# Block-sparse attention and a gated MLP on one core: the order of the first loads and casts, and four groups of transposes

## The chip, the cores and the metric

One Trainium2 chip; the kernel runs on 1 of its cores, in one launch. The metric is the device time of one execution in microseconds, as a median of runs. All inputs lie in HBM as float32, the output goes back to HBM as float32; on the core nearly all products take bf16 operands.

## What is computed

Two layers, one after the other. The first is attention with a block mask, for 4 batches, 8 heads, 768 positions of 64 elements. The mask is the same for all heads; it lets a query block of 32 see its neighbours, the first and last block, and three sampled blocks.

```python
scores = scale * np.matmul(q, k.transpose(0, 1, 3, 2))
...
scores = np.where(mask, scores, -1000000000.0)
attn = softmax(scores)          # over the keys
x = (attn @ v), heads side by side: (4, 768, 512)
```

The second is a gated MLP with a mix over positions:

```python
h = np.maximum(x @ w_in, 0.0)                      # 768 x 1024 per batch
u, v = h[..., :512], h[..., 512:]
v_n = (v - mean(v)) / np.sqrt(var(v) + 1e-06)
v_s = np.einsum('ts,bsd->btd', w_spatial, v_n) + b_spatial[None, :, None]
out = (u * v_s) @ w_out
```

## The kernel before

**Tiles.** Two heads make a pair; there are 16 pairs, four to a batch. `load` (line 103) fetches a pair's k, q or v as 128 partitions x 2 heads x 384 float32 elements (384 KB) into a ring of three buffers for each of the three, and `cast` (115) turns it into bf16: k and q side by side in `nat`, 12 chunks of 128 columns (6 of k, 6 of q), v in `vv` with a column of ones. TensorE transposes `nat` chunk by chunk into PSUM, and VectorE copies it to `kq`, which holds for each of 8 heads 768 columns of k and 768 of q; its 24 further partitions hold the mask rows: block indicators on the k side, 0 or a large negative number on the q side. A score product over 88 rows thus masks as it multiplies. `rows` (239) copies these mask rows from head 0 to other heads.

**Stages.** The first batch (pairs 0 to 3) is worked by units, each a third of the queries (256) of one pair, `UNITS` at line 387; pair 0 is split by heads first. A unit has three slots. In a slot `qk_unit` (390) makes 128x1024 scores by four matmuls and one exponential of ScalarE. `av_unit` (438) follows some slots later with 8 matmuls per slot, and after a unit's third one VectorE normalizes it to `xn`. From slot 36 on heads are worked whole: `qk_full` (413) makes 128x768 scores per slot and `av_full` (465) takes 6 matmuls per slot, seven slots later. The x of a pair has to be transposed once more (`xt`) for the MLP: by TensorE and a copy of VectorE (`xtr_pe`, 485; `xtr_third`, 492, for a unit) or by a DMA transpose on SP's queue (`xtr_dma`, 500). The steps of the MLP (`Moe`, 556) are matmuls into one of two PSUM banks (`moe_tag`, 257, alternates them) and are dealt between the attention's slots by `run_queue` (684). The third batch's MLP runs beside the fourth batch's attention, and the last one by itself at the end.

**Order.** Nothing is scheduled automatically: each engine runs its instructions in program order, and waits are semaphores. The order of a slot is written out in the loop at line 807: scores, then `pre`, then attention products, then the steps under `at` (filled by `when`), then `run_queue`, then `late`. SP issues nearly all loads, stores and DMA transposes, strictly in program order; an issue that has to wait for a buffer holds up all behind it. Two loads of the first pair are issued by ScalarE.

**The start.** Head 0 of pair 0 comes first and in parts: four of six chunks of k and q (`C03`), so that the first scores need little data. The lines that the change touches:

```python
load(0, "k", H0, C03, eng=nc.scalar)
load(0, "q", H0, C03, eng=nc.scalar)
nc.sync.dma_start(out=samp[MR], in_=_listify(sampled_blocks).bitcast(I32))
...
cast(0, "k", nc.scalar, H0, C03)
rows(H1, K_, nc.scalar)
rows(slice(2, 3), slice(0, 512), nc.scalar)
cast(0, "q", PL, H0, C03)
```

`filler` (180) issues matmuls on zeros that are not read. `mask_rows` (272) makes the q side's mask rows for one third of the queries by a matmul and a copy. `split0` (284) copies half of a transposed group to `kq`. `tr_first` (348, slots 4, 7 and 10 for pairs 1, 2 and 3) transposes a pair's six chunks of k and the first two of q; `tr_rest` (356, slots 8, 11 and 14) the other four of q. From pair 4 on k and q are transposed by `tr_dma` (375) and copied by `split` (379), VectorE's copy of `tt` to `kq`.

Of the kernel before, what the change touches and what calls it, by code (L numbers as in the profile page):

```python
# [17 lines left out]
def _listify(ap: bass.AP) -> bass.AP:  # L18
    t = ap.tensor
    if isinstance(t.shape, tuple):  # L20
        t = dataclasses.replace(t, shape=list(t.shape))
        ap = dataclasses.replace(ap, tensor=t)
    return ap
# [3 lines left out]
def kernel(  # L27
# [35 lines left out]
    TC = NCH // NT  # L63
    TW = TC * 128
    S0 = NT * NG * 3
    FILL, FILL2, FILL3 = 26, (6, 0, 2), 4
    U_DVE = (0, 1, 2, 3)

    const = ctx.enter_context(tc.tile_pool(name="const", bufs=1))
# [27 lines left out]
            "h (p c) d -> p h (c d)", c=NCH)[:, :, cs.start * D:cs.stop * D]  # L97

    H0, H1, BOTH = slice(0, 1), slice(1, 2), slice(0, 2)
    ALLC, C01, C03, C45 = slice(0, NCH), slice(0, TC), slice(0, 2 * TC), slice(2 * TC, NCH)  # L100
    SRC = {"k": k, "q": q, "v": v}

    def load(p, nm, hs=BOTH, cs=ALLC, eng=nc.sync):
        if (nm, p) not in st:
            st[nm, p] = work.tile([128, 2, S // 2], FP32, tag="st_" + nm, bufs=3, name="st_" + nm)
        eng.dma_start(out=st[nm, p][:, hs, cs.start * D:cs.stop * D],  # L106
                      in_=dram(SRC[nm], p, hs, cs))
# [7 lines left out]
    def cast(p, nm, eng, hs=BOTH, cs=ALLC):  # L115
        if nm == "v":
            dst = vv[p % NVV][:, hs, cs, 0:D]
        else:
            if p not in nat:
                nat[p] = work.tile([128, 2 * NCH, 2, D], BF16, tag="nat", bufs=4, name="nat")  # L120
            c0 = 0 if nm == "k" else NCH
            dst = nat[p][:, c0 + cs.start:c0 + cs.stop].rearrange("p c h d -> p h c d")[:, hs]
        src = st[nm, p].rearrange("p h (c d) -> p h c d", d=D)[:, hs, cs]
        if p == 0 and nm != "v":
            dst = nat0_view()[:, hs, (c0 + cs.start) * D:(c0 + cs.stop) * D]
            if cs is not C45:
                dst = dst[:, 0].rearrange("p (i t d) -> p t i d", t=2, d=D)
                src = src[:, 0].rearrange("p (t i) d -> p t i d", t=2)
            else:
                dst = dst.rearrange("p h (c d) -> p h c d", d=D)  # L130
        if eng is nc.scalar:
            nc.scalar.activation(out=dst, in_=src, func=AF.Copy)
        else:
            eng.tensor_copy(out=dst, in_=src)  # L134

    samp = const.tile([KR, 2 * NR], I32)
    load(0, "k", H0, C03, eng=nc.scalar)
    load(0, "q", H0, C03, eng=nc.scalar)
    nc.sync.dma_start(out=samp[MR], in_=_listify(sampled_blocks).bitcast(I32))
    load(0, "k", H0, C45)  # L140
    load(0, "k", H1)
    load(0, "q", H1, C03)
    load(1, "k")
    load(1, "q")
    load(0, "v")
    load(2, "k")
    load(2, "q")
    load(1, "v")


# [29 lines left out]
    def filler(n, to):  # L180
        for _ in range(n):
            nc.tensor.matmul(out=to[:, 0:128], lhsT=warm, rhs=warm, start=True, stop=True)
# [56 lines left out]
    def rows(hs, cs, eng=nc.vector):  # L239
        src = kq[MR, 0:1, cs].to_broadcast([NB, hs.stop - hs.start, cs.stop - cs.start])  # L240
        if eng is nc.scalar:
            nc.scalar.activation(out=kq[MR, hs, cs], in_=src, func=AF.Copy)
        else:
            eng.tensor_copy(out=kq[MR, hs, cs], in_=src)

    cast(0, "k", nc.scalar, H0, C03)
    rows(H1, K_, nc.scalar)
    rows(slice(2, 3), slice(0, 512), nc.scalar)
    cast(0, "q", PL, H0, C03)
    cast(0, "k", PL, H0, C45)  # L250
    cast(0, "k", PL, H1)
    cast(0, "q", PL, H1, C03)


# [2 lines left out]
    def moe_tag():  # L257
        moe_tags.rotate(1)
        if moe_tags[0] in held:
            moe_tags.rotate(1)  # L260
        return moe_tags[0]
# [10 lines left out]
    def mask_rows(ps, t0, n, copy, rs=slice(0, KR)):  # L272
        nc.tensor.matmul(out=ps[:, 0:n * TW], lhsT=bm[rs],
                         rhs=kq[rs, 0, t0 * TW:(t0 + n) * TW], start=True, stop=True)
        return lambda: copy(kq[MR, 0, qcols(t0, n)], ps[0:NB, 0:n * TW])


    def head(ps, h, c0, n, at=0):
        for i in range(0, n, 2):
            nc.tensor.transpose(out=ps[:, at + i * 64:at + (i + 2) * 64],  # L280
                                in_=nat0_view()[:, h, (c0 + i) * D:(c0 + i + 2) * D],
                                identity=ident)

    def split0(ps, h, c0, n, t, copy=dve_copy):
        w = n * 64
        copy(kq[0:D, h, c0 * 128 + t * w:c0 * 128 + (t + 1) * w], ps[t * D:(t + 1) * D, 0:w])
# [2 lines left out]
    ps0 = bank()  # L289
    head(ps0, 0, *K4)  # L290
    split0(ps0, 0, *K4, 0)
    split0(ps0, 0, *K4, 1)
    filler(FILL2[0], wps)
    psq = bank("psq", "av")
    head(psq, 0, *Q4)
    split0(psq, 0, *Q4, 0)
    filler(FILL2[1], wps)
    mask_rows(psum.tile([128, 1024], FP32, tag="sc", bufs=2, name="mq"), 0, 1, act_copy)()
    m1 = mask_rows(psum.tile([128, 512], FP32, tag=moe_tag(), bufs=1, name="mq"), 1, 1, act_copy)
    m2 = mask_rows(psum.tile([128, 1024], FP32, tag="sc", bufs=2, name="mq"), 2, 1, dve_copy, MR)  # L300
    filler(FILL2[2], wps)
    split0(psq, 0, *Q4, 1)
    m1()
    m2()
    rows(H1, qcols(0, NT), PL)
    rows(slice(2, 3), slice(512, S), PL)

    cast(1, "k", PL)
    cast(1, "q", PL)
    cast(0, "v", PL)  # L310
    load(3, "k")
    cast(2, "k", PL)
    cast(2, "q", PL)
    cast(1, "v", PL)
    load(3, "q")
    cast(3, "k", PL)
# [175 lines left out]
    def xtr_third(u):  # L492
        t, p = UNITS[u]
        if t == "h":
            if p == 1:
                xtr_pe(0, xn_ref.pop(0), 0, 2 * TC)
        else:
            xtr_pe(p, xn_ref.pop(u), t * TC, TC, x_ref.pop(u))

    def xtr_dma(p):  # L500
        nc.sync.dma_start_transpose(
# [200 lines left out]
        return lambda: f(*a, **kw)  # L702

    K_Q0 = slice(0, S + TW)
    ROWS = [(1, 2, 8, qcols(0)), (1, 3, 4, K_), (5, 4, 6, K_), (6, 6, 8, K_), (14, 4, 8, qcols(1, 2))]
    when(0, second)
    when(1, third)
    when(2, lambda: filler(FILL3, psum.tile([128, 512], FP32, tag=moe_tag(), bufs=1, name="wps")))
# [4 lines left out]
    for p, sl in ((1, 8), (2, 11), (3, 14), (0, 17)):  # L713
        when(sl, c(tr_rest, p, 2 if p == 0 else 1))
    for u in range(1, len(UNITS)):
        late.setdefault({1: 13, 2: 13}.get(u, 3 * u + 7), []).append(c(xtr_third, u))

    def moe_begin(b):
        moe[b] = Moe(b)
# [59 lines left out]
    for p in range(NG, NP):  # L779
        g = slot_of(p)  # L780
        when({4: 14, 5: 22, 6: 31}.get(p, g - 34), c(load, p, "k"), c(load, p, "q"), c(load, p, "v"))
        when({4: 18, 5: 26, 6: 38}.get(p, g - 25),
             c(cast, p, "k", PL), c(cast, p, "q", PL), c(cast, p, "v", PL))
        when({4: 22, 5: 30}.get(p, g - 20), c(tr_dma, p))
        when(g - 5, c(split, p, 0))
        when(g - 3, c(split, p, 1))
        if p == NP - 1:
            when(g + 20, last_x)
        elif p % NG == NG - 1:
            when(g + 20, lambda p=p: xtr_pe(p, xn_ref.pop(("p", p)), 0, NCH))  # L790
        else:
            when(g + 20, c(xtr_dma, p))
    for i, (ld, ca) in enumerate([(16, 19), (16, 21), (17, 23), (17, 25), (23, 27), (23, 29)]):
# [65 lines left out]
```

## Time and profile before

| What | Value |
|---|---|
| Median of 3 runs | 214.83 us (214.56 to 215.42) |
| The profiled execution's own time | 215.21 us |
| Its span on the page | 213.4 us |
| Granted clock of TensorE, mean of the span | 0.99 |
| Busy: PE, ACT, DVE, POOL | 206.6, 171.0, 131.9, 72.9 us |
| DMA | 41.70 MB, mean 195 GB/s |

The profile shows one execution. Times in its views are microseconds from the start of the span unless marked ns. PE is TensorE's matmul row, PEld its weight loads, DVE is VectorE, ACT ScalarE, POOL GpSimd, SP the engine that issues DMAs. A row of a timeline has the start, the length from the first start to the last end, engine, line of the code, operation, out<-in by the program's names, shapes, the number of instructions merged into it, and in brackets the idle time of the engine before it and what ended it. The 1.8 us between span and own time lie around the span and are not resolved.

### The profile page before, as it was taken

To read this page: it belongs to the slowest core of one execution; us is meant where nothing else is said; L and a number is where in the kernel's file an instruction comes from. 1 tells how busy PE (TensorE), PEld (TensorE's weight loads), DVE (VectorE), ACT (ScalarE), POOL (GpSimd) and SP (SyncE) were. 2 spreads that over 40 slices of the span, in tenths; PEclk is the share of its full clock that TensorE was granted. 3 is DMA by queue.
4 is the path that set the end of the run, shared out by engine and by line. 5 is a ranking of instruction groups with operands and counts; after the bars stand their busy time and mean duration, and the time that the engine had idled before them with its cause. 6 is when DMAs were issued, how large, how long until landed. Compare 5 with 4: busy or idle time off the path is not lost.

```text
span 213.4 us, 5299 instructions
## 1 busy us (share of the span) xinstructions
PE 206.6 (97%) x2151; PEld 130.9 (61%) x2151; DVE 131.9 (62%) x287; ACT 171.0 (80%) x226; POOL 72.9 (34%) x119
## 2 busy tenths in 40 slices
PE   8799999999999999999999999999999999999992
PEld 7578887866666665665665565566656656544441
DVE  7589875988854535385887445286784433476551
ACT  6969999999999899979989788978989787266021
POOL 6589669867572405042442040130120000012000
PEclk9969999999999999999999999999999999999999
DMA  5999799999999999999691497697100324610265
GB/s 161 345 342 332 249 316 218 340 191 326 266 375 190 292 191 299 236 280 304 127 259 37 73 289 172 198 307 116 37 3 19 67 52 94 235 55 0 51 172 200
DMA packets 62780, 41.70 MB, mean 195 GB/s; under 512 B 44580, under 2 KB 57508, under 8 KB 62756
## 3 DMA queue, kind: packets, MB, share of 16 engines
q1 hardware_dynamic: 62324, 40.97, 74.7%
q10 hardware_dynamic: 432, 0.39, 0.6%
q8 instruction: 17, 0.28, 0.5%
q14 instruction: 7, 0.06, 0.1%
HBM read 24.38 MB, written 6.29 MB: 144 GB/s over the span
## 4 chain that ended last, share of the span: by engine, by line
PE 92%; DMA 3%; SPq 1%; ACT 1%; POOL 0%; DVE 0%; issue 0%; ACTq 0%
PE ps_moe L546 33%; PE ps L419 22%; PE ps_av L470 13%; PE ps_t L546 7%; PE ps L406 7%; PE ps_av L452 4%; PE ps_sc L546 4%; DMA st_q<-in_q_dram 3%; PE ps L267 1%; SPq L106 1%; PE ps_av L267 1%; ACT osb L217 0%; POOL nat L134 0%; ACT a_all L423 0%; DVE xn L435 0%
## 5 line engine op out<-in xcount | busy, mean ns | idle before, releaser
L423 ACT ACTIVATE a_all<-ps 128x768 bf16<-128x768 f32 x144 | 113.9, 812 | 14.9 <-PE ps L419 7.4
L419 PE MATMUL ps<-kq 88*128 88x384 bf16 x288 | 70.5, 325 | 0.1
L470 PEld LDWEIGHTS <-a_all 128*128 128x128 bf16 x864 | 46.5, 97 | 20.0
L470 PE MATMUL ps_av<-vv,a_all 128*128 128x65 bf16 x864 | 51.2, 194 | 0.0
L419 PEld LDWEIGHTS <-kq 88*128 88x128 bf16 x288 | 28.0, 98 | 31.0 <-issue 0.9
L546 PE MATMUL ps_moe<-w_in_t,xt 128*128 128x512 bf16 x144 | 44.0, 378 | 0.0
L411 ACT ACTIVATE a_all<-ps 128x1024 bf16<-128x1024 f32 x36 | 35.1, 1025 | 3.4 <-PE ps L406 2.9
L546 PE MATMUL ps_moe<-vn,w_spt 128*128 128x512 bf16 x108 | 32.7, 378 | 0.0
L134 POOL CAST nat<-st_k 128x768 bf16<-128x768 f32 (+2 forms) x17 | 13.6, 802 | 41.1 <-DMA st_k<-in_k_dram 40.8
L434 DVE RECIPROCAL rc<-ps_av 128x6 f32<-128x6 f32 (+1 forms) x36 | 6.7, 185 | 28.2 <-PE ps_av L470 26.6
L614 DVE SCALAR_TENSOR_TENSOR un<-ps_moe,b_col,un 128x512 bf16<-128x512 f32 x18 | 13.5, 750 | 16.7 <-PE ps_moe L546 16.1
L406 PE MATMUL ps<-kq 88*128 88x256 bf16 (+1 forms) x140 | 22.9, 286 | 0.7 <-ACT a_all L411 0.7
L583 POOL TENSOR_SCALAR std<-mv 128x3 f32<-128x3 f32 (+1 forms) x9 | 2.1, 238 | 62.2 <-DVE mv L580 45.5
L546 PE MATMUL ps_moe<-w_out_t,gt 128*128 128x512 bf16 x72 | 21.5, 378 | 0.0
L546 PEld LDWEIGHTS <-xt 128*128 128x128 bf16 x192 | 15.4, 97 | 7.2 <-DVE xt L214 0.2
L435 DVE TENSOR_TENSOR xn<-ps_av,rc 128x384 bf16<-128x384 f32 (+1 forms) x36 | 18.5, 513 | 1.2
L579 DVE BATCH_NORM_STATS2 stats<-vn 128x6 f32<-128x512 bf16 x24 | 16.5, 687 | 1.4 <-ACT vn L574 0.9
L134 POOL CAST nat<-st_q 128x768 bf16<-128x768 f32 (+1 forms) x18 | 14.1, 782 | 6.9 <-DMA st_q<-in_q_dram 6.5
L406 PEld LDWEIGHTS <-kq 88*128 88x128 bf16 x140 | 12.8, 100 | 4.6 <-issue 0.8
L134 POOL CAST vv<-st_v 128x768 bf16<-128x768 f32 x16 | 13.6, 855 | 5.7 <-DMA st_v<-in_v_dram 5.6
L452 PEld LDWEIGHTS <-a_all 128*128 128x128 bf16 x288 | 14.2, 100 | 2.0 <-issue 0.7
L214 DVE COPY kq<-tt 64x1536 bf16<-64x1536 bf16 x24 | 15.0, 627 | 0.3
(84 smaller groups left out, 211.8 us busy)
## 6 DMA issues: line engine op xcount, KB each, us to landing
st_v<-in_v_dram SPq DMA_DIRECT2D x16, 384.0 KB, 6.0
out_dram<-osb SPq DMA_DIRECT2D x23, 256.0 KB, 3.1
st_k<-in_k_dram SPq DMA_DIRECT2D x15, 384.0 KB, 4.4
st_q<-in_q_dram SPq DMA_DIRECT2D x15, 384.0 KB, 5.4
ws_f<-in_moe_w_spatial_dram SPq DMA_DIRECT2D x6, 384.0 KB, 6.6
w_f<-in_moe_w_in_dram SPq DMA_DIRECT2D x8, 256.0 KB, 5.9
w_f<-in_moe_w_out_dram SPq DMA_DIRECT2D x4, 256.0 KB, 4.2
st_q<-in_q_dram SPq DMA_DIRECT2D x2, 128.0 KB, 4.7
```

The costliest lines, as they stand in the source:

```text
L134: eng.tensor_copy(out=dst, in_=src)
L214: nc.vector.tensor_copy(out=o, in_=i)
L406: nc.tensor.matmul(out=ps[:, at:at + n * TW], lhsT=kq[:, h, ci * 128:(ci + 1) * 128], rhs=kq[:, h, qcols(t0, n)], start=True, stop=True)
L411: nc.scalar.activation(out=out, in_=ps, func=AF.Exp, scale=0.125)
L419: nc.tensor.matmul(out=ps[:, hf * 512:hf * 512 + HALF], lhsT=kq[:, j % H, ci * 128:(ci + 1) * 128], rhs=kq[:, j % H, S + hf * HALF:S + (hf ...
L423: nc.scalar.activation(out=a_ref["h", j][:, ci, :].rearrange("p (b c) -> p b c", b=2), in_=ps.rearrange("p (b c) -> p b c", b=2)[:, :, 0:H ...
L435: nc.vector.tensor_tensor(out=out, in0=ps[:, :, 0:D], in1=rc[:, 0:n].to_broadcast([128, n, D]), op=ALU.mult)
L452: nc.tensor.matmul(out=av_ref[u][:, to, :], lhsT=a_ref[u][:, at:at + 128], rhs=vv[pp % NVV][:, h, ci, :], start=(ci == 0), stop=(ci == NCH ...
L470: nc.tensor.matmul(out=av_ref[j][:, qc, :], lhsT=a_ref["h", j][:, ci, qc * 128:(qc + 1) * 128], rhs=vv[p % NVV][:, h, ci, :], start=(ci == ...
L546: nc.tensor.matmul(out=ref["ps"][:, 0:w], lhsT=lhs(i), rhs=rhs(i), start=(i == 0), stop=(i == n - 1))
L579: nc.vector.bn_stats(out=stats, in_=self.vn[:, tcc, :])
L614: nc.vector.scalar_tensor_tensor(out=self.un[:, tcc, :], in0=ps, scalar=b_col[:, tcc:tcc + 1], in1=self.un[:, tcc, :], op0=ALU.add, op1=AL ...
```

## The change

Four parts.

1. *Start.* Head 0's first queries are loaded on SP's queue instead of ScalarE's, behind the sampled blocks and ahead of the rest of head 0's keys, and ScalarE casts them instead of GpSimd. ScalarE copies the mask rows of keys to head 1 alone, in two halves of 384 columns around the q-side mask rows; those of head 2 go to VectorE (`ROWS`). GpSimd casts head 1's keys ahead of the last two chunks of head 0's. Four fillers fewer, and VectorE's four copies of `split0` alternate between k and q.
2. *Pair 1's queries.* The first third (two chunks, 128 KB) is loaded and cast by itself; the other two thirds come after pair 2's queries, as a load and as a cast.
3. *x of unit 2* (first third of pair 1): its two transposes move from the end of slot 13 to slot 14, behind that slot's scores.
4. *x of pairs 7 and 11*: the first two chunks are transposed by TensorE, now after the slot's MLP steps, the other four by a DMA on SP. The first `split` of pairs 9 and 13 moves to the end of the next slot.

In the built programs TensorE has 12 matmuls fewer with their weight loads (4 fillers, 8 transposes), SP four DMAs more (the first queries, which ScalarE issued, pair 1's second piece, two transposes), GpSimd one instruction less; the load of pair 3's queries now takes the buffer of pair 2's queries instead of pair 1's.

```diff
-    FILL, FILL2, FILL3 = 26, (6, 0, 2), 4
+    FILL, FILL2, FILL3 = 26, (2, 2), 4
...
-    load(0, "q", H0, C03, eng=nc.scalar)
     nc.sync.dma_start(out=samp[MR], in_=_listify(sampled_blocks).bitcast(I32))
+    load(0, "q", H0, C03)
     load(0, "k", H0, C45)
     load(0, "k", H1)
     load(0, "q", H1, C03)
     load(1, "k")
-    load(1, "q")
+    load(1, "q", cs=C01)
     load(0, "v")
     load(2, "k")
     load(2, "q")
+    load(1, "q", cs=C25)
     load(1, "v")
...
     cast(0, "k", nc.scalar, H0, C03)
-    rows(H1, K_, nc.scalar)
-    rows(slice(2, 3), slice(0, 512), nc.scalar)
-    cast(0, "q", PL, H0, C03)
+    cast(0, "q", nc.scalar, H0, C03)
+    rows(H1, slice(0, 384), nc.scalar)
+    cast(0, "k", PL, H1)
     cast(0, "k", PL, H0, C45)
-    cast(0, "k", PL, H1)
     cast(0, "q", PL, H1, C03)
...
     split0(ps0, 0, *K4, 0)
-    split0(ps0, 0, *K4, 1)
     filler(FILL2[0], wps)
     psq = bank("psq", "av")
     head(psq, 0, *Q4)
+    m0 = mask_rows(psum.tile([128, 1024], FP32, tag="sc", bufs=2, name="mq"), 0, 1, act_copy, MR)
+    m0()
     split0(psq, 0, *Q4, 0)
+    split0(ps0, 0, *K4, 1)
+    m1 = mask_rows(psum.tile([128, 512], FP32, tag=moe_tag(), bufs=1, name="mq"), 1, 1, act_copy, MR)
+    m1()
+    split0(psq, 0, *Q4, 1)
+    m2 = mask_rows(psum.tile([128, 1024], FP32, tag="sc", bufs=2, name="mq"), 2, 1, dve_copy, MR)
     filler(FILL2[1], wps)
...
-    split0(psq, 0, *Q4, 1)
-    m1()
     m2()
+    rows(H1, slice(384, S), nc.scalar)
     rows(H1, qcols(0, NT), PL)
-    rows(slice(2, 3), slice(512, S), PL)
     cast(1, "k", PL)
-    cast(1, "q", PL)
+    cast(1, "q", PL, cs=C01)
     cast(0, "v", PL)
     load(3, "k")
     cast(2, "k", PL)
     cast(2, "q", PL)
+    cast(1, "q", PL, cs=C25)
     cast(1, "v", PL)
     load(3, "q")
...
+    def xtr_rest(p):
+        nc.sync.dma_start_transpose(
+            out=xt_tile(p)[:, 256:].rearrange("p (c n) -> p c n", c=NCH - 2),
+            in_=xn_ref["p", p][:, 2:].rearrange("p c h d -> p (c h d)"))
+
+    def xtr_two(p):
+        xtr_pe(p, xn_ref.pop(("p", p)), 0, 2)
+        moe_tags.rotate(1)
...
-    ROWS = [(1, 2, 8, qcols(0)), (1, 3, 4, K_), (5, 4, 6, K_), (6, 6, 8, K_), (14, 4, 8, qcols(1, 2))]
+    ROWS = [(1, 2, 8, qcols(0)), (1, 2, 4, K_), (5, 4, 6, K_), (6, 6, 8, K_), (14, 4, 8, qcols(1, 2))]
...
     for u in range(1, len(UNITS)):
-        late.setdefault({1: 13, 2: 13}.get(u, 3 * u + 7), []).append(c(xtr_third, u))
+        where, slot = (pre, 14) if u == 2 else (late, 13 if u == 1 else 3 * u + 7)
+        where.setdefault(slot, []).append(c(xtr_third, u))
...
-        when(g - 5, c(split, p, 0))
+        if p % NG == 1 and p > 2 * NG:
+            late.setdefault(g - 4, []).append(c(split, p, 0))
+        else:
+            when(g - 5, c(split, p, 0))
         when(g - 3, c(split, p, 1))
...
         elif p % NG == NG - 1:
-            when(g + 20, lambda p=p: xtr_pe(p, xn_ref.pop(("p", p)), 0, NCH))
+            when(g + 20, c(xtr_rest, p))
+            late.setdefault(g + 20, []).append(c(xtr_two, p))
```

More of the change, by code (lines that the diff above doesn't have):

```diff
@@ L99 @@
     H0, H1, BOTH = slice(0, 1), slice(1, 2), slice(0, 2)
-    ALLC, C01, C03, C45 = slice(0, NCH), slice(0, TC), slice(0, 2 * TC), slice(2 * TC, NCH)
+    ALLC, C01, C03 = slice(0, NCH), slice(0, TC), slice(0, 2 * TC)
+    C25, C45 = slice(TC, NCH), slice(2 * TC, NCH)
     SRC = {"k": k, "q": q, "v": v}
@@ L295 @@
     head(psq, 0, *Q4)
+    m0 = mask_rows(psum.tile([128, 1024], FP32, tag="sc", bufs=2, name="mq"), 0, 1, act_copy, MR)
+    m0()
     split0(psq, 0, *Q4, 0)
-    filler(FILL2[1], wps)
[L298 to L301, printed above, removed]
-    split0(psq, 0, *Q4, 1)
-    m1()
+    split0(ps0, 0, *K4, 1)
[3 more added lines that the diff above has]
+    m2 = mask_rows(psum.tile([128, 1024], FP32, tag="sc", bufs=2, name="mq"), 2, 1, dve_copy, MR)
+    filler(FILL2[1], wps)
     m2()
+    rows(H1, slice(384, S), nc.scalar)
     rows(H1, qcols(0, NT), PL)
-    rows(slice(2, 3), slice(512, S), PL)
     cast(1, "k", PL)
-    cast(1, "q", PL)
+    cast(1, "q", PL, cs=C01)
     cast(0, "v", PL)
```

## The prediction

> **What bounds the kernel now.** I read the page first: share of busy time, clock, chain.
>
> ```profile
> PE 206.6 (97%) x2151; PEld 130.9 (61%) x2151; DVE 131.9 (62%) x287; ACT 171.0 (80%) x226; POOL 72.9 (34%) x119
> ...
> PEclk9969999999999999999999999999999999999999
> ...
> PE 92%; DMA 3%; SPq 1%; ACT 1%; POOL 0%; DVE 0%; issue 0%; ACTq 0%
> ```
>
> TensorE is busy 97% of the span and carries 92% of the chain that ended last; the 3% of DMA in it is one transfer at the start. So two things shorten the kernel: TensorE instructions that go away, and the few stretches in which TensorE stands or runs slowly. The clock row has one such place, its third digit. The table of stretches opens it:
>
> ```profile
> 7.50:11.00 3.50, 2.14 (x22) 1.53 (x21) 1.50 (x5) 3.21 (x4) 1.46 (x3) 0.99 1.05 370
> 11.00:14.40 3.40, 3.40 (x29) 2.23 (x27) 3.19 (x4) 2.05 (x2) 2.82 (x4) 0.50 1.04 354
> 14.40:17.80 3.40, 3.40 (x67) 3.12 (x65) 2.79 (x7) 2.99 (x4) 3.05 (x4) 1.00 1.02 305
> ```
>
> After the length come busy times of PE, PEld, DVE, ACT, POOL, then granted clock, DMA share and GB/s. TensorE is busy 2.14 of 3.50 us, then runs 3.4 us at half clock: 29 matmuls where the next stretch does 67. Why, the timelines of TensorE and of GpSimd tell:
>
> ```profile
> 9.36 0.50 PE L267 MATMUL ps<-ident,nat 128*128 128x128 bf16 x6
> 10.80 0.29 PE L267 MATMUL ps<-ident,nat 128*128 128x128 bf16 x2 [0.94 <-POOL nat L134]
> ...
> 11.88 0.60 PE L452 MATMUL ps_av<-vv,a_all 128*128 128x65 bf16 x8
> 12.29 1.04 PE L406 MATMUL ps<-kq 88*128 88x256 bf16 x4
> ...
> 14.65 0.61 PE L267 MATMUL ps<-ident,nat 128*128 128x128 bf16 x8
> ```
>
> ```profile
> 7.30 0.82 POOL L134 CAST nat<-st_k 128x768 bf16<-128x768 f32 x1
> 9.92 0.83 POOL L134 CAST nat<-st_q 128x768 bf16<-128x768 f32 x1 [1.80 <-DMA st_q<-in_q_dram]
> 10.99 0.83 POOL L134 CAST vv<-st_v 128x768 bf16<-128x768 f32 x1 [0.24 <-DMA st_v<-in_v_dram]
> ...
> 13.07 0.90 POOL L134 CAST nat<-st_q 128x768 bf16<-128x768 f32 x1 [0.20 <-DMA st_q<-in_q_dram]
> ...
> 16.18 0.83 POOL L134 CAST nat<-st_q 128x768 bf16<-128x768 f32 x1 [0.20 <-DMA st_q<-in_q_dram]
> ```
>
> Six transposes of pair 1's keys run, then the two of its queries wait 0.94 us for a cast that waited 1.80 us for its load. From there nearly every cast waits for its own DMA, and they start 1.02 to 1.07 us apart: one 384 KB load per 1.05 us is the pace of supply until 17 us. ScalarE, whose exponentials follow TensorE, stands 1.27, 0.36 and 0.21 us here. After 14.4 us TensorE is never idle for long.
>
> **The change, part by part.** Ready times below are ends of casts: pair 1's q 10.75, pair 0's v 11.82, pair 2's q 13.97, pair 3's q 17.01.
>
> *First queries on SP, cast by ScalarE.* One more issue stands ahead of every SP load after the sampled blocks: 0.43 to 0.47 us per issue in SP's timeline. Where the queue is full (DMA share 1.05) it is hidden, where it was empty it shifts everything: 0 to +0.47, I take +0.3, as the share was only 0.75 to 0.85 between 4 and 6 us. ScalarE pays a cast of 0.40 and saves 512 of its 1,280 mask columns (1.35 us for both copies, so about 0.5); it waits for the load (3.73 at the earliest) instead of GpSimd. Masks then follow as before, the second half of the row copy (0.4) after them, and the first exponential starts near 5.8 instead of 6.02. That, the four fillers fewer (0.06 to 0.11 each), GpSimd's shorter list (0.40 + 0.39) and the head-2 mask rows that go to VectorE (0.82 for both copies now, about 0.2 more) I cost at nothing: the later stands of ScalarE (1.27) and VectorE (2.05) cover them. Without that cover the start would be worth ±0.3.
>
> *A third of pair 1's queries alone.* In the stream 128 KB stand where 384 KB stood. By bytes that is 0.35 instead of 1.05; the page's medians to landing, 4.7 for 128 KB and 5.4 for 384 KB, give the same 0.7. Small runs may cost more, so 0.45 to 0.70 earlier, I take 0.6. With the +0.3: landings 0.3 earlier (0 to 0.7). The cast shrinks to 0.40. Ready: pair 1's third 10.0 (9.6 to 10.3), pair 0's v 11.5 (11.1 to 11.85), pair 2's q 13.65 (13.25 to 14.0). Pair 3's q stands behind the same bytes as before plus one more DMA: 17.3 (17.0 to 17.8).
>
> The Trainium skill speaks against it: "DMA: Bandwidth & Descriptors", section "Rules for kernel authors", says to merge many small transfers into one large one. By it the split only adds overhead and the sum would lose this term; the rows above do show that the consumer needs the first third alone, so I keep the gain.
>
> Now TensorE at full clock. The first attention product of pair 0 starts at 11.55 instead of 11.88. Three groups of 8 (0.26 each) and two of 4 score matmuls (0.44 each, as at 15.1) put it at pair 2's queries near 13.7; that transpose group ends at 13.8 instead of 15.10, 1.3 us earlier. Pair 3's queries were transposed at 18.12, so TensorE comes at 16.8 and waits for 17.3. **0.8 us remain** (0.3 to 1.1).
>
> The clock is the unknown. If it still falls to 0.50 from 11 to 14.4, the same work takes 0.44 and 0.85 per group and only 0.2 us remain. In the 3.5 us before the drop TensorE was busy 2.14; without the 0.94 us it is about 2.9 of 3.5 (83%), and the one neighbour that shows a clock kept is 4 to 7 us, 0.82 to 1.00 busy. So I take the full clock. "TensorE: Matmul & The Clock Gate", section "Why this matters for your kernels", asks for no idle gap above about 3 us. Here a drop follows a longest gap of 0.94 us, so the row speaks against that bound; by the rule the gap would not be the cause, the drop would stay, and the sum would be 0.6 lower.
>
> *The x of unit 2 later* (unit 2 is the first third of pair 1). Its two transposes go behind the next four score matmuls:
>
> ```profile
> 20.83 0.38 PE L267 MATMUL ps<-ident,xn 128*128 128x128 bf16 x4
> 21.46 0.28 PE L267 MATMUL ps_av<-ident,xn 128*128 128x128 bf16 x2 [0.25 <-DVE xn L435]
> ```
>
> Four transposes at 0.055 issue until 21.05, the next two wait for VectorE until 21.46. The score matmuls need only scores that ScalarE has read by then, so **0.41** goes (0.25 at least); nothing is late next, the first product that reads an x starts at 23.2.
>
> *Pairs 7 and 11.* Six transposes become two, the other four chunks an SP DMA; the first two products move ahead of them.
>
> ```profile
> 90.94 0.69 DVE L214 COPY osb<-ps_moe 128x512 f32<-128x512 f32 x1
> ...
> 91.21 0.49 PE L267 MATMUL ps<-ident,xn 128*128 128x128 bf16 x6
> 91.69 0.59 PE L546 MATMUL ps_moe<-w_in_t,xt 128*128 128x512 bf16 x2
> ...
> 92.11 0.49 PE L419 MATMUL ps<-kq 88*128 88x384 bf16 x2
> ```
>
> Before, the products waited until 91.69 for the bank that VectorE's copy frees at 91.63. Now they take the free bank at 91.21, two products of 0.215 end at 91.64, two transposes of 0.055 follow: scores at 91.79, 0.32 earlier. Pair 11 alike (139.99, scores at 140.84): 0.31. Together 0.63. Against it stands the DMA: SP issues it after the two output stores, at 94.09, and such transposes land 2.7 to 5.4 us after issue, 96.8 to 99.5; the third value block reads these columns in its sixteenth step, at 97.7. So a wait of 0 to 1.8 us; pair 11 0 to 1.5. Median landing is 2.8, but stores and loads share the queue: I take 0.15 each. **0.33** (-1 to 0.63). Behind the new DMA on SP stand the loads of a later pair (cast several slots later) and one transpose of nat; neither is due. VectorE's split copies of pairs 9 and 13 (0.55) go one slot later, three slots ahead of their reader: nothing.
>
> Sum: 0.8 + 0.41 + 0.33 = 1.54 us. The profiled execution took 215.21, so 213.67; it lies 0.38 above the median 214.83 of the runs, so 213.3 as a median.
>
> **The rivals.**
>
> *Pair 3's queries come late, the slow side.* Their load now takes the buffer of pair 2's queries and waits on SP until that cast ends: issued at 13.7 instead of 10.77, with pair 3's v, four more loads and all of w_in behind it. At the page's 5.4 us it lands at 19.1, is cast at 20.0, and TensorE is 1.9 us later than before; minus 0.74 this is +1.15: 216.0, and more if the clock falls again. It decides at 3.5 us from issue to landing: beyond that the start loses. For it: the median. Against it: much of that median is time in a full queue, and the first 128 KB loads landed 2.2 to 2.5 us after issue; this load has to be there only when pair 3's keys ahead of it are done, about 15.5.
>
> *The half clock stays.* 0.2 + 0.41 + 0.33 = 0.94: 213.9.
>
> *The supply lag goes.* Between the casts at 7.30 and 9.92 lie 2.6 us where later steps take 1.05; if the order of loads dissolves that 1.5 us lag, no transfer stops TensorE and the start gains 1.3 to 1.6: 212.5.
>
> **How the numbers follow.** Forecast 0.42 (213.3), lag gone 0.20 (212.5), half clock 0.22 (213.9), late queries 0.16 (216.0). About 0.5%, 1.07 us, is what a measurement of this kernel tells from no change: faster means under 213.76, slower over 215.90. Faster: 0.37 of the forecast's 0.42 (its low bounds end above), 0.20 of the lag and 0.03 of the half clock: 0.60. Slower: 0.12 of the late queries. The rest, 0.28, is no change. The range reaches from below the lag's 212.5 to a half clock with a waiting DMA, 215.1; it leaves out most of the late queries and a little below: 212.2 to 215.1.
>
> **What would show it.** Right: no 0.94 us wait before pair 1's last two transposes, clock 1.00 from 11 to 14.4, a wait of about 0.5 us for pair 3's cast near 17, two products ahead of two transposes near 90 and 138 us, no wait of them for xt later. Wrong: the clock row still low, pair 3's cast after 18, products that wait for the xt DMA, or a first exponential after 6.3.

## The result and the profile after

Slower, where faster was forecast. The median of 6 runs is **217.8 us** (215.04 to 220.49) against 214.46 us (213.7 to 215.42) for the kernel before on the same chip; the ratio is **1.0107** (95% interval 1.0072 to 1.0142), about 2.3 us. Executions over 1.5% above the fastest of the same kernel (two of the six here, both with a lower granted clock) are left out of the ratios here and below, not out of the medians and ranges, so a ratio does not price a wait that comes in a few executions. The profiled execution took 218.22 us with a span of 216.2; the one before had 215.21 and 213.4.

The page after, its rows of PE, of the clock and of the chain:

```profile
PE 205.2 (95%) x2139; PEld 129.7 (60%) x2139; DVE 131.9 (61%) x287; ACT 171.0 (79%) x227; POOL 74.5 (34%) x118
...
PEclk9999999999999999999999999999999999999999
...
PE 70%; DMA 15%; SPq 6%; POOL 3%; DVE 1%; issue 1%; ACT 1%; ACTq 0%
```

TensorE works 1.4 us less and the half clock of the third digit is gone, as forecast. But TensorE holds 70% of the chain instead of 92%: 15% is now DMA, 6% SP's issues, 3% GpSimd. Nearly a quarter of the chain now goes through transfers, their issue and GpSimd.

The same three stretches as before (columns as there, the last but one is the DMA share):

```profile
7.50:11.00 3.50, 2.66 (x32) 1.84 (x30) 3.18 (x7) 3.50 (x5) 2.44 (x4) 1.00 0.96 309
11.00:14.40 3.40, 3.13 (x53) 2.61 (x49) 3.30 (x6) 3.21 (x4) 3.09 (x4) 1.00 0.88 298
14.40:17.80 3.40, 3.00 (x53) 2.69 (x54) 2.74 (x7) 2.27 (x4) 2.65 (x4) 1.00 0.90 280
```

TensorE does 53 matmuls in the second stretch where it did 29. The other change is in the DMA column: 0.88 and 0.90 where before had 1.04 and 1.02. SP's timeline tells why:

```profile
7.20 0.81 SPq L107 DMA_DIRECT2D st_k<-in_k_dram  x1
12.82 0.37 SPq L107 DMA_DIRECT2D st_q<-in_q_dram  x1
13.24 1.24 SPq L107 DMA_DIRECT2D st_v<-in_v_dram  x1
...
15.55 1.42 SPq L226 DMA_DIRECT2D w_f<-in_moe_w_in_dram  x3
```

From 8.0 to 12.82 us SP issues nothing: the load of pair 3's queries waits for the cast that frees its buffer (it was issued at 10.77 before). The first load of `w_in` follows at 15.55 instead of 12.72. In the kernel before:

```profile
10.77 0.37 SPq L106 DMA_DIRECT2D st_q<-in_q_dram  x1
...
12.72 9.76 SPq L224 DMA_DIRECT2D w_f<-in_moe_w_in_dram  x8
```

At 48 us TensorE is 0.94 us ahead of before (the 43rd exponential starts at 47.73 instead of 48.67). Then it loses 1.81 us in one place. GpSimd, VectorE and TensorE there:

```profile
45.93 3.55 POOL L531 CAST ws_b<-ws_f 128x256 bf16<-128x256 f32 x6 [2.05 <-DMA w_spt<-ws_b]
49.56 0.23 POOL L595 TENSOR_SCALAR std<-mv 128x2 f32<-128x2 f32 x1
49.87 0.73 POOL L597 TENSOR_TENSOR rstd<-std,mhalf 128x2 f32<-128x2 f32 x1
```

```profile
50.63 0.41 DVE L190 TENSOR_SCALAR vn<-vn,mv,rstd 128x512 bf16<-128x512 bf16 x1 [2.71 <-POOL rstd L597]
50.96 1.18 DVE L216 COPY kq<-tt 64x1536 bf16<-64x1536 bf16 x1
52.06 0.91 DVE L190 TENSOR_SCALAR vn<-vn,mv,rstd 128x512 bf16<-128x512 bf16 x1
52.89 0.67 DVE L190 TENSOR_SCALAR vn<-ps_moe 128x512 bf16<-128x512 f32 x1
```

```profile
51.62 0.36 PE L472 MATMUL ps_av<-vv,a_all 128*128 128x65 bf16 x6
53.62 0.38 PE L558 MATMUL ps_moe<-w_in_t,xt 128*128 128x512 bf16 x1 [1.64 <-DVE vn L190]
```

The same places in the kernel before:

```profile
44.74 3.55 POOL L519 CAST ws_b<-ws_f 128x256 bf16<-128x256 f32 x6 [2.83 <-DMA w_spt<-ws_b]
...
48.69 0.73 POOL L585 TENSOR_TENSOR rstd<-std,mhalf 128x2 f32<-128x2 f32 x1
```

```profile
49.45 0.41 DVE L188 TENSOR_SCALAR vn<-vn,mv,rstd 128x512 bf16<-128x512 bf16 x1 [0.60 <-POOL rstd L585]
...
51.71 0.67 DVE L188 TENSOR_SCALAR vn<-ps_moe 128x512 bf16<-128x512 f32 x1
```

```profile
52.75 0.38 PE L546 MATMUL ps_moe<-w_in_t,xt 128*128 128x512 bf16 x1
```

GpSimd's third pair of spatial-weight casts waits for a buffer that a transposing DMA (`w_spt`) has to empty. It did so before as well, but the buffer now comes free 1.19 us later (45.93 instead of 44.74). Behind these casts, in program order, stand `std` and `rstd` of the MLP. VectorE waits 2.71 us for `rstd` (0.60 before), and behind its `vn` steps stands the one that reads the MLP's PSUM bank (`vn<-ps_moe`). When that ends, at 53.56, the bank is free, and TensorE goes on at 53.62. All of the chain is 1.18 us later than before (`rstd` ended at 49.42, now at 50.60), TensorE is 0.94 us earlier, and before had 0.31 us to spare (bank free at 52.38, TensorE there at 52.75, less the same 0.06 from one to the other): 1.18 + 0.94 - 0.31 = 1.81.

The second place is pair 7's x, 2.51 us; TensorE, then SP:

```profile
98.38 0.38 PE L558 MATMUL ps_moe<-w_in_t,xt 128*128 128x512 bf16 x1
101.10 0.39 PE L558 MATMUL ps_moe<-w_in_t,xt 128*128 128x512 bf16 x1 [2.34 <-DMA xt<-xn]
```

```profile
91.09 2.76 SPq L379 DMA_TRANSPOSE tt<-nat  x1
93.94 1.46 SPq L664 DMA_DIRECT2D out_dram<-osb  x2
95.50 1.21 SPq L504 DMA_TRANSPOSE xt<-xn  x1
```

The new DMA is issued at 95.50 (forecast 94.09), behind a transpose of twelve chunks and two stores, and lands at 101.06. Fifteen of its sixteen DMA engines were done by 99.70, which alone would have made about 1.1 us of wait; the last one took 1.36 us more. A 16 KB instruction fetch ran from 99.03 to 99.98. It may have stood in front of that last one, but the trace does not say on which engine it ran. Pair 11's landed at 148.13, 1.2 us ahead of its reader.

The account: 0.94 ahead at 48 us, 0.32 and 0.31 won at pairs 7 and 11, 1.81 and 2.51 lost: 2.75 us slower; the spans differ by 2.8.

### The profile page after: what moved, and what is told of

The parts are those of the page before. It is cut to its first block, busy times and chain, and to the rows that moved or that the text cites. A ratio compares the mean times of both kernels' runs of the same rounds, so it can differ in the third digit from the quotient of the medians.

```text
span 216.2 us, 5286 instructions
## 1 busy us (share of the span) xinstructions
PE 205.2 (95%) x2139; PEld 129.7 (60%) x2139; DVE 131.9 (61%) x287; ACT 171.0 (79%) x227; POOL 74.5 (34%) x118
## 4 chain that ended last, share of the span: by engine, by line
PE 70%; DMA 15%; SPq 6%; POOL 3%; DVE 1%; issue 1%; ACT 1%; ACTq 0%
PE ps_moe L558 27%; PE ps L421 19%; PE ps_av L472 12%; PE ps_t L558 7%; SPq L107 4%; DMA w_spt<-ws_b 4%; PE ps_sc L558 3%; DMA st_q<-in_q_dram 3%; DMA st_v<-in_v_dram 3%; DMA w_f<-in_moe_w_in_dram 3%; DMA xt<-xn 3%; POOL ws_b L531 2%; DVE vn L190 1%; POOL w_in_t L232 1%; DVE kq L216 1%
## 5 line engine op out<-in xcount | busy, mean ns | idle before, releaser
L425 ACT ACTIVATE a_all<-ps 128x768 bf16<-128x768 f32 x144 | 114.0, 813 | 18.6 <-PE ps L421 11.2
L472 PEld LDWEIGHTS <-a_all 128*128 128x128 bf16 x864 | 46.4, 97 | 20.0
L408 PE MATMUL ps<-kq 88*128 88x256 bf16 (+1 forms) x140 | 21.6, 275 | 1.0 <-DVE kq L216 0.6
L591 DVE BATCH_NORM_STATS2 stats<-vn 128x6 f32<-128x512 bf16 x24 | 16.5, 687 | 1.4 <-ACT vn L586 0.9
L190 DVE TENSOR_SCALAR vn<-vn,mv,rstd 128x512 bf16<-128x512 bf16 x24 | 12.6, 560 | 5.9 <-POOL rstd L597 5.9
L135 POOL CAST nat<-st_q 128x768 bf16<-128x768 f32 (+2 forms) x18 | 14.9, 833 | 3.5 <-DMA st_q<-in_q_dram 3.3
L216 DVE COPY kq<-tt 64x1536 bf16<-64x1536 bf16 x24 | 15.8, 659 | 0.5 <-DMA tt<-nat 0.2
```

Of the source, the lines that this page charges most:

```text
L190: nc.vector.tensor_scalar(out=out, in0=in0, scalar1=s1, scalar2=s2, op0=o0, **kw)
L216: nc.vector.tensor_copy(out=o, in_=i)
L408: nc.tensor.matmul(out=ps[:, at:at + n * TW], lhsT=kq[:, h, ci * 128:(ci + 1) * 128], rhs=kq[:, h, qcols(t0, n)], start=True, stop=True)
L425: nc.scalar.activation(out=a_ref["h", j][:, ci, :].rearrange("p (b c) -> p b c", b=2), in_=ps.rearrange("p (b c) -> p b c", b=2)[:, :, 0:H ...
L472: nc.tensor.matmul(out=av_ref[j][:, qc, :], lhsT=a_ref["h", j][:, ci, qc * 128:(qc + 1) * 128], rhs=vv[p % NVV][:, h, ci, :], start=(ci == ...
L591: nc.vector.bn_stats(out=stats, in_=self.vn[:, tcc, :])
```

## The experiments

Theory A: these two waits hold the loss, and SP's wait for a staging buffer makes the first. Against it: the loss is the new start's own; TensorE's lead makes the wait whatever SP does; or the pairs alone are to blame. In the table, the first part of each name says what is built on: `no_` and `after_` on the kernel after, `best_` on the best combination, the others on the kernel before. Ratios are to the kernel before in the same job.

| Kernel | median us | ratio, 95% interval |
|---|---|---|
| first_only (part 1) | 214.73 | 1.0001 (0.9982 to 1.0020) |
| split_only (part 2) | 214.66 | 1.0001 (0.9982 to 1.0020) |
| unit2_only (part 3) | 214.33 | 0.9977 (0.9958 to 0.9995) |
| pairs_only (part 4) | 213.73 | 0.9956 (0.9927 to 0.9984) |
| split_unit2 (2, 3) | 214.52 | 1.0009 (0.9983 to 1.0034) |
| no_pairs (1, 2, 3) | 215.95 | 1.0063 (1.0035 to 1.0090) |
| no_pairs_4buf | 214.42 | 0.9999 (0.9981 to 1.0017) |
| no_pairs_wsb3 | 214.45 | 1.0011 (0.9990 to 1.0033) |
| after_4buf | 215.23 | 1.0002 (0.9967 to 1.0038) |
| after_wsb3_tt | 215.26 | 0.9982 (0.9959 to 1.0006) |
| after_4buf_wsb3_tt | 213.58 | 0.9938 (0.9914 to 0.9962) |
| pairs_tt | 214.08 | 0.9973 (0.9952 to 0.9993) |
| **best_tt** (3, 4 and two fixes) | **213.04** | **0.9931 (0.9909 to 0.9954)** |
| best_split | 214.88 | 0.9976 (0.9947 to 1.0005) |
| best_split_4buf | 213.37 | 0.9949 (0.9920 to 0.9977) |
| best_first | 214.16 | 0.9969 (0.9948 to 0.9990) |
| best_first_fill | 214.16 | 0.9989 (0.9964 to 1.0013) |
| best_six | 214.10 | 0.9990 (0.9969 to 1.0011) |

**The parts alone.** No part loses alone; the sum of the four ratios is -0.65%, and the whole is +1.07%. So the loss lies in how they meet.

*pairs_only*: the kernel before with part 4 of the diff alone.

> The kernel before with the change at pairs 7 and 11 alone. Theory A (the kernel after lost 2.51 us at 98.4 us because the transposing DMA for pair 7's x is issued behind a transpose of nat and two output stores, and lands after the sixteenth step of the products): the same wait shows here, 1 to 3 us in one place between 96 and 102 us, less the 0.6 us that the two products won; a net loss of 0.5 to 2.4 us, 215.0 to 216.9. Theory B (the loss is in the start; the pairs do what was forecast): 0.33 us faster, 214.1, with no wait above 0.3 us between 90 and 105 us.

The median is 213.73, even below theory B's 214.1, and in its trace there is hardly a wait for `xt`: the DMA was issued at 92.07 and landed at 96.25, and the sixteenth step came at 96.29, 0.07 us late. Theory A as I put it here is wrong: the DMA is not late by itself. But its 12 runs reach to 218.82, those of the kernel before in the same job to 216.72. The trace has one more lesson, since its start is that of the kernel before, instruction for instruction:

```profile
11.00:14.40 3.40, 3.16 (x56) 2.66 (x52) 3.30 (x6) 3.28 (x4) 2.84 (x4) 1.00 1.08 375
```

No half clock, 56 matmuls, and TensorE waited 0.17 us for pair 1's cast, not 0.94. The 43rd exponential starts at 47.15: 1.52 us earlier than in the profile that I forecast from, with the same code.

*unit2_only*: the kernel before with part 3.

```diff
-        late.setdefault({1: 13, 2: 13}.get(u, 3 * u + 7), []).append(c(xtr_third, u))
+        where, slot = (pre, 14) if u == 2 else (late, 13 if u == 1 else 3 * u + 7)
+        where.setdefault(slot, []).append(c(xtr_third, u))
```

> The kernel before with only unit 2's x transposed later. The forecast was 0.41 us faster: 214.1. From the kernel before's trace the chain through GpSimd's rstd leaves only 0.31 us at 52 us, so 0.3 at most: 214.2 to 214.5, with VectorE's wait for rstd at 49 us grown to about 1 us. If it gives nothing, 214.5, the transposes' wait of 0.41 us was covered by something else late in the start.

0.5 us (0.1 to 0.9) and no wait left between 17 and 22 us. VectorE waited 1.05 us for `rstd`, yet TensorE did not wait near 52: the slack there is no fixed 0.31 us. It depends on whether a cast of GpSimd has started when VectorE's copy of `kq` starts. In the kernel after the cast started 0.13 us ahead of the copy, and the copy took 1.18 us. In no_pairs_wsb3 no cast ran, and it took 0.55. In split_only the copy started 0.06 us ahead and took 0.55, and the cast took 1.18 instead of 0.83. The Trainium skill has the reason ("SBUF — State Buffer", section "Who interferes with whom": VectorE and GpSimd share one port pair under an exclusive lock); these durations agree with it.

*split_only* and *first_only*: parts 2 and 1 of the diff alone; the loads of part 2 (its casts alike):

```diff
-    load(1, "q")
+    load(1, "q", cs=C01)
     load(0, "v")
     load(2, "k")
     load(2, "q")
+    load(1, "q", cs=C25)
```

> The kernel before with only pair 1's queries split: a third alone, the other two thirds loaded and cast after pair 2's queries. Theory F (the split is what blocks SP: the load of pair 3's queries must then wait for a cast of pair 2's queries instead of pair 1's): that load is issued at about 12.8 us instead of 10.77, the first w_in load at 14.5 or later, GpSimd's rstd ends at 50 or later, and TensorE waits 0.5 to 1.8 us near 52 us: 215.0 to 215.9. Theory G (the loss of the start is in the first queries on SP and ScalarE and in the fewer fillers): no wait near 52 us and a time within 0.4 of before, 214.1 to 214.9.

> The kernel before with only the first queries on SP and cast by ScalarE, the masks and fillers as in the kernel after; pair 1's queries in one piece. Theory F: the first w_in load is issued at 13 us or before, no wait above 0.3 us near 52 us, 214.1 to 214.9. Theory G: a wait near 52 us or a late start, 215.3 or more.

Theory F was right on the mechanism and wrong on the price. In split_only pair 3's query load is issued at 12.30, the first `w_in` load at 15.30; in first_only that is 11.57. But `rstd` ended at 49.25, TensorE was at its 43rd exponential at 48.03 only, and nothing waited near 52. TensorE has to be early *and* the chain late.

*split_unit2*: both of these edits.

> The kernel before with pair 1's queries split and unit 2's x later, nothing else. Theory K (a race: the split makes rstd 1 to 2 us later, unit 2 makes TensorE 0.4 us earlier, each alone within the slack, together beyond it): VectorE waits 1.4 us or more for rstd, TensorE 0.2 to 0.9 us near 52 us, 214.4 to 215.0. Theory L (the loss of no_pairs needs the first queries on SP as well): no wait above 0.2 us near 52 us and unit 2's gain kept, 214.1.

Neither theory: VectorE waited 1.55 us for `rstd` (49.97), TensorE not at all near 52; unit 2's gain was gone already in the start, in a wait of 0.86 us for pair 3's queries at 16.8.

**The first wait.** *no_pairs* undoes part 4; *no_pairs_4buf* and *no_pairs_wsb3* add one buffer each:

```diff
-            st[nm, p] = work.tile([128, 2, S // 2], FP32, tag="st_" + nm, bufs=3, name="st_" + nm)
+            st[nm, p] = work.tile([128, 2, S // 2], FP32, tag="st_" + nm, bufs=4 if nm == "q" else 3, name="st_" + nm)
...
-            ws["b", i // 2] = work.tile([128, 2, NCH, 128], BF16, tag="ws_b", bufs=2, name="ws_b")
+            ws["b", i // 2] = work.tile([128, 2, NCH, 128], BF16, tag="ws_b", bufs=3, name="ws_b")
```

> The kernel after with pairs 7 and 11 as before; the new start and unit 2's later x are kept. Theory A: TensorE is 0.93 us earlier at 48 us, then waits 1.8 us near 52 us for VectorE's vn, which waits for GpSimd's rstd, so 0.9 us slower than before: 215.3 (214.9 to 215.8), and no wait near 98 us. Theory C (all of the loss comes from pairs 7 and 11, the wait near 52 us is made up later): 0.9 us faster than before, 213.5.

> As no_pairs, with four buffers instead of three for staged queries, so that the load of pair 3's queries need not wait on SP for a cast of pair 2's. Theory A: the loads behind it (value loads, w_in, the spatial weights) are issued about 2 us earlier, at 12.7 us or before for the first w_in load instead of 15.55; GpSimd's rstd comes at 48.7 or before instead of 49.87 and the wait near 52 us shrinks from 1.8 to below 0.8 us; before had only 0.31 us of slack there, so the gain of the start is mostly eaten: 214.1 (213.5 to 214.4). Theory D (TensorE's being earlier alone makes the wait, SP's block has no part): the wait stays at 1.5 us or more, 215.3.

> As no_pairs, with three buffers instead of two for the cast spatial weights, so that GpSimd's third pair of casts need not wait for the landing of the first transposing DMA of them. Theory A (rstd is late because it stands behind these six casts in GpSimd's order): rstd is there before 48 us, the wait near 52 us goes, and the start's 0.93 us is kept: 213.5 (213.2 to 213.9). Theory E (the late loads themselves, the staged spatial weights or the statistics, bind the same step): the wait stays above 1 us, 215.3.

The mechanism is theory A's on all three, but its times were too low: 215.95 against 215.3, 214.42 against 214.1, 214.45 against 213.5. no_pairs waits 1.82 us at 52.4, as the kernel after does, and nowhere near 98. With a fourth staging buffer the first `w_in` load goes out at 11.20 instead of 16.08 and the wait is gone. The stretches of no_pairs, then of no_pairs_4buf:

```profile
10.30:14.40 4.10, 3.86 (x56) 3.17 (x55) 3.46 (x6) 4.10 (x5) 2.99 (x4) 1.00 0.82 272
14.40:18.00 3.60, 3.29 (x58) 2.91 (x57) 3.28 (x8) 3.15 (x4) 2.57 (x4) 1.00 0.86 257
```

```profile
10.30:14.40 4.10, 3.06 (x53) 2.62 (x49) 3.97 (x7) 3.93 (x5) 3.77 (x5) 1.00 1.07 380
14.40:18.00 3.60, 3.32 (x59) 3.13 (x60) 3.35 (x8) 2.52 (x3) 3.22 (x4) 1.00 1.07 365
```

The DMA share falls from 1.07 to 0.82 and 0.86 where SP waits: (0.25 x 4.1 + 0.21 x 3.6) = 1.8 us of DMA time are not used. With a third `ws_b` buffer instead, the SP wait stays (first `w_in` load at 15.28), but GpSimd no longer waits. Its `rstd` row and VectorE's `vn`:

```profile
46.73 0.73 POOL L597 TENSOR_TENSOR rstd<-std,mhalf 128x2 f32<-128x2 f32 x1
```

```profile
47.68 0.40 DVE L190 TENSOR_SCALAR vn<-vn,mv,rstd 128x512 bf16<-128x512 bf16 x1
48.00 0.55 DVE L216 COPY kq<-tt 64x1536 bf16<-64x1536 bf16 x1
```

No wait of VectorE and none of TensorE. So both links are shown, the missing staging buffer and the cast queue ahead of `rstd`. But neither kernel is faster than before: with the wait gone, no gain of the start comes to light.

**The second wait.** *after_4buf* is the whole change with four staging buffers.

> The whole change, with four buffers for staged queries instead of three. Theory F: the wait near 52 us goes as in no_pairs_4buf (214.4), and the pairs' gain comes on top as it did alone (0.9 us): 213.5 (213.2 to 213.9). Theory H (with this start the transposing DMA of pair 7 is late against TensorE whatever SP does early on): a wait of 1 to 2.5 us near 98 us remains and the time stays at 215 or above.

Between both: 1.0002. The profile still has 0.50 us near 52 and 0.61 us at 97.6, and a wait of 1.41 us for pair 3's queries at 16.5, whose cast waited for its load though SP did not hold it up. The runs spread from 213.29 to 217.55. The next three move the transposes of pairs 10's and 14's `nat` behind the new DMA, and have three `ws_b` buffers (*pairs_tt* not):

```diff
-        when({4: 22, 5: 30}.get(p, g - 20), c(tr_dma, p))
+        when({4: 22, 5: 30, 10: 93, 14: 141}.get(p, g - 20), c(tr_dma, p))
```

> The kernel before with the change at pairs 7 and 11 alone, as pairs_only, and the transposes of pairs 10's and 14's nat issued behind the new DMA. Theory A (the new DMA is late because it queues behind a transpose of twelve chunks): issued within 1.5 us of the first two products, it lands at least 1 us ahead of the sixteenth step; the median 213.5 (213.2 to 213.8), and the scatter of pairs_only (213.09 to 218.82) shrinks to below 2.5 us. Rival J (the moved transposes are then late for VectorE's split, or instruction fetches delay the DMA all the same): a new wait near 101 us or the same scatter, 214 or more.

> The whole change, with the two obstacles removed that its trace shows: three buffers for the cast spatial weights (GpSimd's rstd no longer behind a wait for a transposing DMA), and the transposes of pairs 10's and 14's nat issued behind the new DMA for pair 7's and 11's x instead of ahead of it. Theory A (these two places hold all that was lost): no wait above 0.3 us near 52 us nor between 90 and 105 us, and what unit 2 (0.5) and the pairs (0.9) gave alone comes through, with nothing from the start: 213.2 (212.8 to 213.6). Theory I (the new start itself costs): 214.3 or more without such waits.

> The start of the kernel before, with unit 2's later x, the change at pairs 7 and 11 with the nat transposes behind the new DMA, and three buffers for the cast spatial weights. If the gains add up, 0.5 + 0.9 to 1.1 us: 213.1 (212.7 to 213.4). If the start of the kernel after is worth its 0.8 us, after_wsb3_tt is 0.5 us or more below this one; if not, the two are alike.

pairs_tt keeps its 12 runs within 213.03 to 214.97 (theory A), but its median is 214.08 where 213.5 was expected, not lower than that of pairs_only. best_tt adds up as expected and beats both kernels. It has only six runs, and one of them took 217.32, so the risk may not be gone. The chain of its profile (213.45):

```profile
PE 90%; DVE 6%; ACT 2%; issue 0%; ACTq 0%
```

No DMA and no SP in it. after_wsb3_tt, which differs from it by the start alone, does not get there: 1.55 us of wait for pair 3's queries at 16.4, 0.93 us at 97.2, runs up to 219.86. Its DMA for pair 7 was issued at 92.31 (best_tt: 91.16) but landed at 98.29 (94.30). What stands ahead of it is late: SP issues the load of pair 11's values at 89.81, in best_tt at 86.34, in pairs_only at 86.53, in the kernel after at 89.92, while TensorE in after_wsb3_tt is only 0.6 us behind best_tt there (84.37 and 83.77 at the 85th exponential). That looks like SP's wait of the first 15 us, still there after 75 us, and the twenty traces fit it. In the seven in which the first `w_in` load goes out at 14.9 or later, all with the split and three staging buffers, the load of pair 11's values is issued at 89.01 to 89.92; in the other thirteen, with 11.2 to 13.1, at 85.82 to 88.97. The queue has little room to catch up: from 40 to 100 us the DMA share is 1.12 to 1.19 in every 20 us of the kernel after.

**The start once more, on best_tt.** *best_split* adds the split, *best_split_4buf* also the fourth buffer, *best_first* part 1 alone, *after_4buf_wsb3_tt* everything.

> best_tt with pair 1's queries split (three buffers, so SP waits). Theory M: first w_in load at 15 us or later, DMA share below 0.95 in one of the stretches from 10 to 18 us, pair 7's x issued more than 0.5 us later than in best_tt, a wait near 97 us in part of the runs: 214.0 (213.4 to 214.8). Rival N (the split is harmless here, the first queries cost): 213.0 as best_tt.

> best_split with four buffers for staged queries. Theory M: no hole, first w_in load before 13 us, 213.0 (212.6 to 213.4), as best_tt or a little faster by what the earlier third of pair 1 gives. If the split itself (more and smaller DMAs, pair 3's queries behind more of them) costs: 213.6 or more with SP not waiting.

> best_tt with the first queries on SP and cast by ScalarE, masks and fillers as in the kernel after; pair 1's queries whole. Theory M: no hole, as best_tt within 0.4 us, 213.0 (212.6 to 213.4). Rival N: 213.8 or more.

> after_wsb3_tt with four buffers for staged queries: the whole change with all three obstacles removed. Theory M: no wait near 52 or 97 us in most runs, 213.0 (212.5 to 213.5). If the start of the kernel after were worth its forecast 0.8 us on top of best_tt: 212.3. If something else in the combined start costs: 214 or more.

best_split spreads from 212.94 to 217.86. Its profiled execution (217.64) has the wait for pair 7's x and what can follow it; TensorE's row and two stretches:

```profile
99.44 0.39 PE L558 MATMUL ps_moe<-w_in_t,xt 128*128 128x512 bf16 x1 [2.35 <-DMA xt<-xn]
```

```profile
97.50:101.00 3.50, 1.56 (x15) 0.94 (x16) 1.10 (x2) 0.85 (x2) 0.00 (x0) 0.99 1.16 199
101.00:104.40 3.40, 3.40 (x21) 1.69 (x20) 0.47 (x2) 2.22 (x4) 2.68 (x4) 0.50 1.09 296
```

After the wait the clock falls to 0.50 for 3.4 us, which costs TensorE another 1.7 us. The load of pair 11's values went out at 89.59, the DMA at 92.16, and landed at 99.39. With four buffers the ratio is 0.9949. The whole change with all three remedies has 0.9938, 213.0 by the ratio (median 213.58, of 7 runs): close to the 213.3 forecast for the change alone, but no better than best_tt, which lacks parts 1 and 2.

For the split theory M fits: above 215.9 us lie 10 of the 24 runs of best_split and after_wsb3_tt, which have three staging buffers, and 2 of the 17 of the same two kernels with four (the intervals of the ratios overlap). But a late issue is not the whole cause of the second wait. The profile of after_4buf_wsb3_tt (216.2) has it too, although its DMA was issued as early as best_tt's:

```profile
91.19 2.26 SPq L504 DMA_TRANSPOSE xt<-xn  x1
```

```profile
99.21 0.39 PE L558 MATMUL ps_moe<-w_in_t,xt 128*128 128x512 bf16 x1 [2.76 <-DMA xt<-xn]
```

It landed at 99.16, 8.0 us after its issue, best_tt's after 3.1. Just before the landing the transfers hardly moved; best_split's stretch first, then that of after_4buf_wsb3_tt (share next to last):

```profile
98.00:99.00 1.00, 0.00 (x0) 0.00 (x0) 0.00 (x0) 0.00 (x0) 0.00 (x0) 1.00 0.06 6
```

```profile
98.00:99.00 1.00, 0.00 (x0) 0.00 (x0) 0.00 (x0) 0.00 (x0) 0.00 (x0) 1.00 0.16 28
```

In both an instruction fetch had begun about 2.2 us ahead of the landing (97.18 and 96.98), and packets of 256 bytes that started between 97.4 and 97.9 took up to 1.51 us. That the fetch holds them up is not shown, and what does stays open.

For part 1 theory M does not fit: 0.9969, about 0.8 us slower than best_tt where 0.4 at most was expected (the intervals just overlap).

*best_first_fill* puts the four fillers back (`FILL2` = (6, 2)), since in 4 of 9 traces with part 1 TensorE came to full clock only after 9 us, and in none of 10 with the old start.

> best_first with eight filler matmuls in the start as in the kernel before, instead of four. If the missing fillers let TensorE come late to full clock: full clock before 7 us, first exponential at 6.2 us or before, and 213.1 (212.7 to 213.5), as best_tt. If the fillers do not matter: 213.7 (213.4 to 214.3), as best_first.

Full clock at 5.4 us, but 0.9989: putting the fillers back wins no time, so they are not the cause. What part 1 costs stays open; with the split and four buffers it costs nothing that shows.

*best_six* has the two products first, but all six transposes on TensorE, with unit 2's edit and three `ws_b` buffers:

```diff
+    def xtr_six(p):
+        xtr_pe(p, xn_ref.pop(("p", p)), 0, NCH)
+        moe_tags.rotate(1)
```

> The kernel before with unit 2's x later, three buffers for the cast spatial weights, and at pairs 7 and 11 the first two products ahead of the transposes, but all six transposes on TensorE and no DMA. From the kernel before's trace the order alone is worth about 0.14 us per pair (the wait between transposes and products), the DMA another 0.2 us each: so 0.5 + 0.3 us faster, 213.8 (213.5 to 214.1), 0.4 to 0.7 us slower than best_tt's 213.04, with no wait near 97 us and a highest run below 215.5. If the DMA brings nothing, it is as fast as best_tt.

0.9990, where 0.8 us less was expected: the order alone is worth nothing. From the 85th to the 97th exponential, across pair 7's transposes, it takes 11.07 us, the kernel before 11.08, best_tt and pairs_only 10.77. The gain is the DMA's, and so, it seems, is the risk: best_six's highest run is 215.20. Unit 2's 0.5 us, which best_six has too, lies within its interval but does not show by itself.

## Why the prediction was wrong

**Right.** No wait of 0.94 us, clock 1.00 from 11 to 14.4. TensorE's wait for pair 3's queries at 16.9: 0.44 us against 0.5 forecast; that cast ended at 16.89 against 17.3. Their load landed 3.2 us after its issue, within the 3.5 that the rival set as the limit. That the wait met the forecast so closely is luck in part: in other traces of the whole new start it is between nothing that shows (after_4buf_wsb3_tt) and 1.55 us (after_wsb3_tt). The first exponential at 5.88 (5.8). Unit 2: 0.5 us alone (0.41). The pairs' own gain: 0.32 and 0.31 us (0.32 and 0.31).

**The step that failed.** I priced SP's wait for the buffer of pair 2's queries by pair 3's queries alone. The rival named what stands behind it ("pair 3's v, four more loads and all of w_in") and gave it no price. It is the price: 1.8 us of unused DMA time, `rstd` 1.18 us later at 50 us, so 1.81 us of wait for TensorE, which the runs with a fourth staging buffer or a third `ws_b` buffer remove; and SP's queue at 90 us, 1.9 us later than in the trace of before and 3.4 than in that of pairs_only. The split's -0.6 became a loss as soon as TensorE ran ahead. Before's trace would have shown it: the VectorE row at 49.45 with a wait of 0.60 us for `rstd`, and DMA shares of 1.09 to 1.15 from 40 to 100 us.

**A term mis-sized.** The wait for the xt DMA, 0.15 us each, 0 to 1.8 at most: 2.51 us at pair 7, none at pair 11. The bound took the issue from before's queue (94.09; it was 95.50, as the same change makes SP late) and 2.7 to 5.4 us to landing from other transposes; the eleven traces with this DMA have 3.1 to 8.0 at pair 7. Why a landing takes 8.0 us stays open.

**A base that was not typical.** The start's 0.8 us was worked out from an execution with a lagging DMA engine and a half clock. Of pair 1's queries fifteen DMA engines landed by 8.20 us and the last one at 9.87; in pairs_only this was 8.30 and 8.81. The mean clock of that execution is 0.99; of the 158 executions of the kernel before that were measured beside the experiments one has 0.989, all others 0.995 or more. pairs_only, pairs_tt and unit2_only, with the same loads and casts, keep the full clock; their 43rd exponentials lie at 47.15, 47.70 and 47.02 us, those of seven traces with the whole new start (unit 2's edit in it) between 46.87 and 48.35. My rival "the supply lag goes" described what the kernel before does in most of these traces.

**The rules weighed.** The rule on small transfers spoke against the split for a reason that does not show here: with a fourth buffer the same smaller DMAs cost nothing that shows (no_pairs_4buf 0.9999). On the clock, the last section.

## What to carry over

Where the DMA share is near or above 1 for tens of microseconds, an issue that waits on an in-order queue can make the later transfers late for long (here it still shows after 75 us); ask what the last consumer of that stream is, not only the next. Before speeding up one engine, read how long the others already wait for each other a little later (0.60 us for `rstd` here): that is the slack which the gain will meet. Parts that are each harmless alone can lose together, so measure them in pairs, and read a second trace of the same code before pricing a stall of the first few microseconds.

## What the runs showed of the hardware

- A fetch of 16 KB of instructions (16 in the kernel after, 0.92 to 1.53 us each) goes over the DMA engines too. One ran while pair 7's DMA landed, and one of 16 engines landed 1.36 us after the others; that the fetch was the cause fits the times, but is not shown. The Trainium skill ("Runtime: NRT & Kernel Launch", section "Instruction fetch mechanics") calls the cost of crossing such a block mostly hidden; no run here measures that cost by itself.
- After a wait of 2.35 us the clock fell to 0.50 in best_split; it stayed at 1.00 after one of 2.34 us in the kernel after and one of 2.76 us in after_4buf_wsb3_tt; before's fell after 0.94 us. The length of the wait does not decide; what does was not found.
